# An instruction order planned by the kernel, quadrant tiles, and statistics turned on VectorE in a fused linear-attention and SoLU kernel

## The chip, the cores and the metric

The kernel runs on one core of a Trainium2 chip. The metric is the device time of one execution in microseconds (us). A run counts as slow when it lies over 1.5% above the fastest of the same kernel, and as fast otherwise. Times quoted are medians of all runs, ratios use fast runs alone.

A few names. PE is TensorE (matmuls), PEld its weight loads, DVE is VectorE, ACT is ScalarE, POOL is GpSimd, which also issues the loads, and SP issues the stores. PSUM is the memory that PE writes its products to; the kernel divides it into eight tiles of 128 x 512 fp32, called *banks* here. Each engine has a queue of instructions, waits on semaphores for the others, and takes its queue in the given order: in the kernel before, PE stands 7.03 us before a product whose operand has not landed (at 25.1 us), although operands of a later product in its queue were ready at 19.3. The *granted clock* is the share of full speed that PE was allowed to run at.

## The reference

```python
# batch 8, heads 8, sequence 576, head dim 64: 4608 tokens of 512
def attention(q, k, v, g_norm):
    kv = einsum('bhsd,bhse->bhde', k, v)          # no softmax: 64 x 64 per head
    out = einsum('bhsd,bhde->bhse', q, kv)
    rms = sqrt(mean(out * out, axis=-1) + 1e-06)   # over the 64 of one head
    return out / rms * g_norm

def feed_forward(x, w_in, w_out, g_ln):            # w_in 512 x 1024, w_out 1024 x 512
    h = x @ w_in
    e = exp(h - max(h)); sm = e / sum(e)
    solu = h * sm
    ln = (solu - mean(solu)) / sqrt(var(solu) + 1e-06) * g_ln
    return ln @ w_out
# the heads of the attention's result are put side by side to form x
```

All inputs and the output are float32.

## The kernel before

The tokens are worked in nine chunks of 512: chunk c below 8 is the first 512 tokens of batch c, chunk 8 the eight remainders of 64. For one chunk the kernel makes kv, turns q, multiplies q @ kv, divides by the root mean square (x), then makes h = x @ w_in, e = exp(h), u = h e, the sums of u, u² and e over the 1024 columns, and u @ w_out, scaled at the end by one number per token. w_out is centred beforehand: the column means weighted with g_ln are subtracted, so that the mean of u need not be.

These are the parts that the change touches:

```python
# loads: 512 rows of k, v, q per batch, and remainders of 64 rows on their own, in 128 B pieces
def load_rem(t, src, b):
    lo = (b % 2) * 64
    nc.gpsimd.dma_start(t[lo:lo + 64, b // 2], src[b, :, 512:S, :].rearrange("h s d -> s h d"))

# q @ kv: one matmul of K = 128 per head pair, with kv on the diagonal of a 128 x 128 tile, zeros beside it
nc.tensor.matmul(t[:, :], kvbd[:, c, p, :], q_sb[c][:, p, :], start=True, stop=True)

# statistics: 20 matmuls into four column groups, an eviction, and four fp32 matmuls that turn the sums
for n, (i, mov) in enumerate(todo):                 # 8 of u², 8 of u, 4 of e
    j = n % 4
    nc.tensor.matmul(t[32 * j:32 * j + 32, :], stat_sel[:, i, :], mov, ..., tile_position=(0, 32 * j))
nc.vector.tensor_copy(sums[:, :], t[:, :])
for m in range(4):
    nc.tensor.matmul(st_ps[:, m, :], sums[:, m * 128:(m + 1) * 128], stat_pick[:, :], ...)

# column means of w_out in full fp32
for f in range(NF):
    nc.tensor.matmul(mean[0][:, :], g_mean[:, f, :], w_out_f[:, f, :], ...)

# the order: each step of chunk c has slots 0 to 7; the other work is put into slots by hand,
# and the framework's scheduler may still move it
at(0, 2, kv_mm, 1)
...
for c in range(NC):
    for m in range(4):
        at(c + 1, 2 * m, out_half, c, m, 0)
        at(c + 1, 2 * m + 1, out_half, c, m, 1)
    at(c + 1, 1, stats, c)
```

The softmax here doesn't subtract the row's maximum and nothing guards it: scores larger than these inputs give would overflow.

## Time and profile before

| what | before |
|---|---|
| median time (3 runs) | 233.3 us (231.86 to 233.44) |
| span of the profiled run | 231.9 us |
| start of the column sums of chunk 0 | 61.15 us |
| stretches of chunks 1 and 2, sums to sums | 23.0 and 22.0 us |
| the three full chunks after those | 20.2 us each |
| sums of the last chunk to the end | 14.4 us |

The nine places where a chunk's column sums start on PE serve as landmarks throughout: from one to the next lies one chunk's worth of work. The prediction shows the busy time of each engine between them. Two rows of finer stretches, 65 to 75 us, come from the table of busy time by stretches: the stretch and its length, busy time and instruction count of PE, PEld, DVE, ACT and POOL, then PE's granted clock, the DMA share and GB/s.

```profile
65.00:70.00 5.00, 3.46 (x53) 2.20 (x53) 3.60 (x7) 3.20 (x7) 4.96 (x6) 0.94 1.63 178
70.00:75.00 5.00, 4.67 (x35) 1.92 (x35) 3.79 (x7) 3.30 (x7) 5.00 (x7) 0.71 1.41 190
```

POOL is full in both and PE has a gap of 1.5 us in the first; right after that the granted clock falls to 0.71 in the mean of 5 us. Cut finer, it is 0.50 from 69.6 to 72.8 us and 1.00 on both sides.

Two rows of the groups of instructions (line, engine, operation, shapes, count; busy time in all, mean ns of one) belong to the statistics before:

```profile
L253 DVE COPY sums<-sum_ps 128x512 f32<-128x512 f32 x9 | 6.2, 692 | 8.3 <-PE sum_ps L248 8.3
L264 DVE TENSOR_TENSOR sq<-st 128x8 f32<-128x8 f32 x9 | 4.6, 509 | 0.3
```

The eviction of the sums takes 692 ns. An operation on eight numbers per partition takes 509 ns on average.

### The profile page before, as it was taken

The numbers are of one execution on the slowest core, as the hardware profiler recorded it, in microseconds if no ns is written. First come the engines' busy times: TensorE is split into PE (matmuls) and PEld (weight loads), VectorE is DVE, ScalarE is ACT, GpSimd is POOL, SyncE is SP. The second block draws the span as 40 slices with busy tenths as digits, with TensorE's granted clock in tenths as the row PEclk, the third lists the DMA queues.
The fourth block names the chain that finished last, engine by engine and source line by source line (L and its number), as shares of the span: only waits on it lengthen the run. The fifth ranks groups of instructions, "written<-read, shape, count | busy, mean of one in ns | idle before, by whom it ended". The sixth has DMA issues, their size and how long they took to land.

```text
span 231.9 us, 3917 instructions
## 1 busy us (share of the span) xinstructions
PE 197.1 (85%) x1510; PEld 95.6 (41%) x1536; DVE 142.3 (61%) x254; ACT 120.9 (52%) x199; POOL 159.6 (69%) x165
## 2 busy tenths in 40 slices
PE   0241679997979998999999999999999999999971
PEld 0230343443444434445444544544455454454330
DVE  4320161579677756965975696597668758557341
ACT  2003452656467556576667657666667848624110
POOL 8643200999999999998658476665847757869500
PEclk9999999999997999999999999999999999999998
DMA  5999999399999999999211021021102202202225
GB/s 60 178 197 198 258 316 190 40 139 116 195 178 193 223 219 169 138 174 183 88 52 45 3 90 71 24 90 48 47 0 102 82 0 93 91 0 91 93 60 122
DMA packets 45682, 27.00 MB, mean 116 GB/s; under 512 B 14944, under 2 KB 40544, under 8 KB 45664
## 3 DMA queue, kind: packets, MB, share of 16 engines
q0 software_dynamic: 39216, 17.30, 57.5%
q1 hardware_dynamic: 6448, 9.44, 12.6%
q8 instruction: 12, 0.20, 0.4%
q14 instruction: 6, 0.05, 0.1%
HBM read 32.51 MB, written 9.44 MB: 181 GB/s over the span
## 4 chain that ended last, share of the span: by engine, by line
PE 58%; POOL 15%; DMA 13%; DVE 6%; ACT 4%; issue 3%; POOLq 0%
PE out_ps L283 21%; PE h_ps L226 18%; DMA w_out_f<-in_moe_w_out_dram 8%; POOL usq_sb L235 5%; DMA vs<-in_v_dram 4%; PE sum_ps L248 4%; PE mean_ps L305 4%; PE st_ps L260 3%; POOL es_sb L237 3%; PE s_ps L207 3%; PE qT_ps L181 2%; DVE sq L264 2%; POOL ks L73 2%; POOL qs L73 2%; ACT osq L203 2%
## 5 line engine op out<-in xcount | busy, mean ns | idle before, releaser
L235 POOL TENSOR_TENSOR usq_sb<-u_sb 128x512 bf16<-128x512 bf16 x72 | 75.0, 1044 | 32.8 <-DVE u_sb L234 32.5
L233 ACT ACTIVATE e_sb<-h_ps,zero_t 128x512 f32<-128x512 f32 x72 | 48.9, 684 | 60.0 <-PE h_ps L226 59.6
L226 PE MATMUL h_ps<-x_sb,w_in_sb 128*128 128x512 bf16 x279 | 76.0, 387 | 1.9 <-DVE x_sb L212 0.8
L283 PE MATMUL out_ps<-w_out_sb,u_sb 128*128 128x512 bf16 x274 | 72.5, 379 | 2.7 <-DVE ob L291 1.4
L234 DVE TENSOR_TENSOR u_sb<-h_ps,e_sb 128x512 bf16<-128x512 f32 x72 | 49.4, 688 | 36.0 <-ACT e_sb L233 36.0
L237 POOL TENSOR_TENSOR es_sb<-e_sb 128x512 bf16<-128x512 f32 x36 | 45.9, 1274 | 14.2 <-ACT e_sb L233 13.8
L226 PEld LDWEIGHTS <-w_in_sb 128*128 128x128 bf16 x288 | 27.9, 101 | 38.0 <-issue 10.7
L283 PEld LDWEIGHTS <-u_sb 128*128 128x128 bf16 x288 | 26.4, 98 | 32.6 <-issue 3.7
L203 ACT ACTIVATE osq<-o_ps,zero_t 128x512 bf16<-128x512 f32 x36 | 24.1, 679 | 16.3 <-remote 14.8
L212 DVE SCALAR_TENSOR_TENSOR x_sb<-o_ps,g_rep,rst 128x512 bf16<-128x512 f32 x36 | 26.8, 749 | 7.8 <-ACT rst L211 7.3
L209 ACT ACTIVATE lss<-s_ps,eps_t 128x512 f32<-128x512 f32 x36 | 24.4, 682 | 8.3 <-PE s_ps L207 8.2
L291 DVE TENSOR_SCALAR ob<-out_ps,rstd 128x512 f32<-128x512 f32 x36 | 26.1, 743 | 3.0 <-PE out_ps L283 2.3
L211 ACT ACTIVATE rst<-lss,zero_t 128x512 f32<-128x512 f32 x36 | 25.8, 721 | 2.3 <-DVE x_sb L212 1.4
L181 PE MATMUL qT_ps<-ident,qs 128*64 128x128 bf16 x256 | 12.5, 246 | 10.9 <-POOL ident masks.py:199 8.4
L181 PEld LDWEIGHTS <-qs 128*64 128x64 bf16 x256 | 9.5, 124 | 18.1 <-issue 9.0
L167 DVE CAST kvbd<-kv_ps 64x256 bf16<-64x256 f32 x16 | 6.7, 419 | 14.9 <-PE kv_ps L158 14.7
L207 PE MATMUL s_ps<-osq,head_mean 128*128 128x512 bf16 x36 | 14.4, 405 | 1.7 <-ACT osq L203 1.3
L149 PE MATMUL kv_ps<-vs,ks 128*64 128x64 bf16 x256 | 7.3, 210 | 8.7 <-DMA vs<-in_v_dram 8.6
L186 DVE COPY qT_sb<-qT_ps 128x1024 bf16<-128x1024 bf16 x18 | 12.3, 683 | 2.5 <-PE qT_ps L181 2.4
L196 PE MATMUL o_ps<-qT_sb,kvbd 128*128 128x512 bf16 x29 | 11.3, 405 | 2.9 <-DVE x_sb L212 1.5
L149 PEld LDWEIGHTS <-ks 128*64 128x64 bf16 x256 | 5.9, 123 | 17.3 <-issue 17.3
L253 DVE COPY sums<-sum_ps 128x512 f32<-128x512 f32 x9 | 6.2, 692 | 8.3 <-PE sum_ps L248 8.3
(49 smaller groups left out, 138.5 us busy)
## 6 DMA issues: line engine op xcount, KB each, us to landing
out_dram<-ob SPq DMA_DIRECT2D x32, 256.0 KB, 2.5
qs<-in_q_dram POOLq DMA_DIRECT2D x8, 512.0 KB, 8.6
ks<-in_k_dram POOLq DMA_DIRECT2D x8, 512.0 KB, 8.3
vs<-in_v_dram POOLq DMA_DIRECT2D x8, 512.0 KB, 9.8
w_out_f<-in_moe_w_out_dram POOLq DMA_DIRECT2D x1, 2048.0 KB, 19.2
w_in_sb<-in_moe_w_in_dram POOLq DMA_DIRECT2D x2, 512.0 KB, 12.4
out_dram<-ob SPq DMA_DIRECT2D x8, 128.0 KB, 2.3
krem<-in_k_dram POOLq DMA_DIRECT2D x8, 64.0 KB, 7.6
```

The source lines that it names most:

```text
L181: nc.tensor.transpose(t[hh * 64:hh * 64 + 64, pp, cols], qs[c][:, 2 * p + hh, j, :], ident[:, :])
L203: nc.scalar.activation(out=osq[:, :], in_=t[:, :], func=AF.Square, bias=zero_t[:, :])
L209: nc.scalar.activation(out=lss[:, :], in_=t[:, :], func=AF.Ln, bias=eps_t[:, :])
L211: nc.scalar.activation(out=rst[:, :], in_=lss[:, :], func=AF.Exp, scale=-0.5, bias=zero_t[:, :])
L212: nc.vector.scalar_tensor_tensor(out=x_sb[c][:, p, :], in0=o_ps.pop((c, p))[:, :], scalar=g_rep[:, :], in1=rst[:, :], op0=MUL, op1=MUL)
L226: nc.tensor.matmul(t[:, :], w_in_sb[:, dt, f * 128:(f + 1) * 128], x_sb[c][:, dt, :], start=(dt == 0), stop=(dt == NP - 1),)
L233: nc.scalar.activation(out=e[:, f % 2, :], in_=t[:, :], func=AF.Exp, bias=zero_t[:, :])
L234: nc.vector.tensor_tensor(out=u_sb[c][:, f, :], in0=t[:, :], in1=e[:, f % 2, :], op=MUL)
L235: nc.gpsimd.tensor_tensor(out=usq_sb[c][:, f, :], in0=u_sb[c][:, f, :], in1=u_sb[c][:, f, :], op=MUL)
L237: nc.gpsimd.tensor_tensor(out=es_sb[c][:, f // 2, :], in0=e[:, 0, :], in1=e[:, 1, :], op=ADD)
L283: nc.tensor.matmul(t[:, :], u_sb[c][:, f, m * 128:(m + 1) * 128], w_out_sb[:, f, :], start=(f == 0), stop=(f == NF - 1),)
L291: nc.vector.tensor_scalar_mul(out=ob[:, :], in0=t[:, :], scalar1=rstd_sb[c][:, m:m + 1])
```

## The change

The intent is to take instructions off PE, to relieve POOL, and to start earlier, with an order of instructions that the kernel plans itself:

- A planner (a greedy list scheduler with one duration per piece) fixes the order, and the framework's scheduler is off.
- k and v are loaded as 96 partitions of six rows, with no remainder; q's remainders sit in their own tile.
- q @ kv uses 64 x 64 quadrants of the PE array: no zero half.
- The sums are turned by DVE's 32 x 32 block transpose and four small fp32 matmuls per chunk.
- The column means use the reduced fp32 type.
- Two of eight squares of u move from POOL to ACT; matmuls on zeros keep PE busy during the first loads; banks are shared out anew.

```diff
+FP32R = mybir.dt.float32r
+class Plan:                                  # pieces with engine, length, rank, needs and buffers
+    def order(self):                         # earliest start first, then the lowest rank
...
+    ctx.enter_context(tc.manual_schedule())
+    banks = {"h": 2, "out": 2, "o": 2, "s": 1, "misc": 1}
...
-    w_out_f = big.tile([128, NF, d_model], FP32, name="w_out_f")
+    w_out_f = big.tile([128, NF, d_model], FP32R, name="w_out_f")
...
+    plan.add("warm", "pe", 5.2, -9.0, lambda: warm(12), first=[("s", "warm")])
...
+    def load_kv(name, src, b):
+        t = T[name, b] = tile_of((name, b), [S // 6, H, 6, D], BF16)
+        nc.gpsimd.dma_start(t.rearrange("p h i d -> p h (i d)"), src[b].rearrange("h (p i) d -> p h (i d)", i=6))
...
+                for hh in range(2):
+                    for z in range(2):
+                        rows = slice(64 * z, 64 * z + 64)
+                        nc.tensor.matmul(
+                            ts[z][hh * 64:hh * 64 + 64, pp, :, cols], kvd[rows, b, hh, 2 * hf + pp, :],
+                            T["qT", c, hf][rows, 2 * pp + hh, :, cols], start=True, stop=True)
...
+    def sums(c, part):                       # u, u², e: three pieces of the plan, not one
+        ...
+    def sums_turn(c):
+        nc.vector.transpose(t.rearrange("p a b c -> p (a b c)"), T["sum", c][:, :])
+    def stats_mm(c):
+        for g in range(4):
+            nc.tensor.matmul(t[32 * g:32 * g + 32, :, :], fold[:, :], T["sumT", c][:, :, g, 0:3], ...)
...
+            engine = "act" if f in (2, 6) and c > 1 else "pool"      # squares of u
...
+            dst = out.rearrange("(b s) d -> b s d", b=B)[:, 512:S, :].rearrange("b (p j) d -> j b p d", j=4)
...
+    for c in range(NC):
+        for part in range(3):
+            plan.add(("sums", c, part), "pe", (0.5, 0.5, 0.25)[part], r + 0.1 + 0.02 * part, ...)
```

## The prediction

> **What bounds the kernel now.** I read the page's engine shares first, then the table of busy time by stretches, then the timelines. The page says only that PE is the busiest engine and that POOL is second:
>
> ```profile
> PE 197.1 (85%) x1510; PEld 95.6 (41%) x1536; DVE 142.3 (61%) x254; ACT 120.9 (52%) x199; POOL 159.6 (69%) x165
> ```
>
> An average over stages hides the limits, so I cut the span at the nine places where the column sums of a chunk start (tile sum_ps in PE's timeline: 61.15, 84.15, 106.15, 126.34, 146.55, 166.73, 185.75, 203.19, 217.54). Columns: stretch, its length, then busy time of PE, PEld, DVE, ACT, POOL.
>
> ```profile
> 61.15:84.15 23.00, 20.81 (x179) 9.93 (x181) 16.36 (x27) 15.35 (x26) 22.90 (x26) 0.93 1.54 198
> 84.15:106.15 22.00, 20.35 (x171) 9.81 (x174) 15.62 (x26) 13.15 (x23) 21.90 (x24) 1.00 1.28 170
> 106.15:126.34 20.19, 19.96 (x170) 9.79 (x172) 14.56 (x26) 13.25 (x23) 14.18 (x14) 1.00 0.37 92
> ...
> 185.75:203.19 17.44, 17.25 (x111) 8.27 (x113) 11.75 (x21) 11.09 (x19) 12.86 (x12) 1.00 0.17 61
> 203.19:217.54 14.35, 14.29 (x84) 6.72 (x84) 9.27 (x16) 4.61 (x8) 11.64 (x12) 1.00 0.15 55
> 217.54:231.90 14.36, 7.92 (x52) 3.53 (x52) 4.27 (x9) 0.59 (x2) 0.60 (x1) 0.93 0.39 93
> ```
>
> The kernel has four regimes. From 106 to 217 us PE is full (19.96 of 20.19) and nothing else is: PE sets the rate, 20.2 us a chunk. From 61 to 106 us POOL is full (22.90 of 23.00): it squares u, adds e, and also issues loads; PE has gaps, and in the row 65 to 70 its granted clock fell to 0.94, in 70 to 75 to 0.71. Before 61 us lies the start, and the end has PE half idle. PE's timeline of the start and of the end:
>
> ```profile
> 13.68 1.07 PE L149 MATMUL kv_ps<-vs,ks 128*64 128x64 bf16 x32 [1.55 <-DMA vs<-in_v_dram]
> ...
> 25.11 0.29 PE L149 MATMUL kv_ps<-vs,ks 128*64 128x64 bf16 x3 [7.03 <-DMA vs<-in_v_dram]
> 25.34 0.61 PE L207 MATMUL s_ps<-osq,head_mean 128*128 128x512 bf16 x1
> ```
> ```profile
> 31.81 1.03 PE L226 MATMUL h_ps<-x_sb,w_in_sb 128*128 128x512 bf16 x2
> 33.06 1.06 PE L226 MATMUL h_ps<-x_sb,w_in_sb 128*128 128x512 bf16 x2 [0.22 <-DVE qT_sb L186]
> 34.68 3.75 PE L305 MATMUL mean_ps<-w_out_f,g_mean 128*128 128x512 f32 x4 [0.56 <-DMA w_out_f<-in_moe_w_out_dram]
> ```
> ```profile
> 220.92 1.02 PE L283 MATMUL out_ps<-w_out_sb,u_sb 128*128 128x512 bf16 x4
> 223.36 3.61 PE L283 MATMUL out_ps<-w_out_sb,u_sb 128*128 128x512 bf16 x16 [1.42 <-DVE ob L291]
> ```
>
> At the start, the squares of chunk 0 are ready by 19.3 us (ACT's four squares run 16.84 + 2.42), but the instruction order puts the kv product of batch 1 ahead of their head sums, and that waits until 25.1 for v of batch 1. So the first h matmul is at 31.8; then the fp32 column means take 8.9 us of PE (the chain's pieces 3.75+0.86+1.72+2.59), in h's way. At the end PE waits 1.42 us for a bank.
>
> **What the Trainium skill says.** "TensorEngine Tiling (Array Packing)", Tiling Modes / Key Properties, says that different tiles run matmuls in parallel and that a change of tiling mode drains the array. The trace agrees: 32 kv matmuls of 64 columns take 0.62 us on the chain, 19 ns each, where 64 columns at h's pace (512 in the 0.216 us below) would need 27 ns alone; and the 20 sums matmuls of 512 columns in four column groups take 1.19 us where 20 in a row at the 0.216 us seen for h (a start to start of 0.86 us for four) would take 4.3. No run yet shows quadrants (row and column halves together). "FP8 and Floating Point Precision", TensorE Precision Notes, gives true fp32 four passes and a reduced fp32 with truncation. The trace: 16 fp32 instructions for 8 calls, 8.9 us, 1.1 us per call or five times 0.216. "VectorE: DVE Perf Modes", The three transpose paths, says that DVE transposes in 32x32 blocks only, so the change needs its extra `fold` matmul; nothing in this trace shows its cost. "DMA: Bandwidth & Descriptors", Specifications, asks for at least 512 B a packet; before, 14944 packets are smaller, but the rows show 190 GB/s written as bf16 in every loading stretch, with or without remainders, so I expect little from larger packets.
>
> **The change, part by part (PE work of one steady chunk).**
> - h and out: unchanged, 64 x 0.216 = 13.8 us. s (head sums): 4 x 0.216 = 0.87, unchanged.
> - Sums 1.2: unchanged, though split in three.
> - q turns: 32 transposes of 64 weights took 2 x 0.57 = 1.14; now 16 of full width. The remainder chunk shows that form: 8 in 0.45. So 0.90. Saved 0.24.
> - o = q @ kv: 4 x 0.216 = 0.87; now 16 quadrant matmuls of 256 columns. Four at a time: 4 x 0.107 = 0.43, and a switch of mode in each half, about 0.1 (the kv and sums groups have gaps of that size about them): 0.55. Saved 0.3. The zero half of kv and its memsets go.
> - kv: 40 matmuls in 0.62 + 0.25 = 0.87; now 48 with K=96, at 19 ns 0.93. Lost 0.06. Its four copies are split over DVE and ACT (about 0.42 each by the present row).
> - Statistics: 8 fp32 instructions, 0.80; now a DVE transpose replaces the eviction copy (0.69 the same size, if it streams one element a cycle) and 4 small fp32 calls, about 0.25. Saved 0.55.
> Sum: 20.2 - 0.24 - 0.3 + 0.06 - 0.55 = **19.1 us a chunk**, if no other engine takes over.
>
> **The other engines in that chunk.** POOL: usq 6 x 1.044 (two squares go to ACT) + es 4 x 1.274 = 11.4, loads 3 x 0.92 and one q remainder 0.72 = 3.5: 14.9 us, from 13.5 + 5.0 = 18.5 before. ACT: 8 e + 12 of o + 2 squares at the 0.58 start to start of its timeline, 2 copies, rstd: 14.2. DVE: 8 x 0.62 + 4 x 0.67 + 4 x 0.67 + 2 x 0.62 + 2 x 0.4 + 0.6 + 1.0 = 14. All under 19.1, so PE stays the bound, and POOL stops being one.
>
> **The start.** v of batch 0 now lands with its remainder: 0.2 MB more is ahead of it, while the small packets behind it go, so about 14 us as now (13.7). kv 1.0, copies 0.9, q@kv 0.5: o at 16.5. Then ACT does 2 squares, 4 Ln, 4 Exp, 10 x 0.6 = 6 us with about 0.8 of filling, and the last x_mul 0.75: first h at **24**, from 31.8, because nothing waits for batch 1 in between. In chunk 0, ACT has 8 e and 12 of attention(1), 12 us, plus waits; DVE 8 u, 4 x, copies and 8 w_center of 0.74, 15 us, part of it after w_out lands (34.6 before; same bytes, so 33); POOL 13.5 + 2.8. PE has only 12. So chunk 1's h starts near 38 (before 53.3, found by counting 32 h matmuls), and sums(0) falls at about 42 instead of 61.15: **19 us gained**, of which 8 is the earlier first h, 7 the fp32r means (8 x 0.22 = 1.8 for 8.9), 4 the denser order. The warming matmuls use idle PE time and only keep early durations near 0.38 rather than 0.61 us.
>
> **The span, landmark by landmark.** sums(0) 42; +20.0 for chunk 1, which still has late w_center work on DVE (before 23.0): 62; +19.3 (before 22.0, POOL bound): 81.3; three at 19.1 (before 20.2): 138.6; the remainder chunk's stretch 18.4 (before 19.0; its q@kv in 128 small matmuls gives some back): 157.0; 16.9 (17.44): 173.9; 13.8 (14.35): 187.7; tail 12.8 (14.36: less the 1.42 wait, as the last two outputs use other banks, and one store instead of eight half stores): **200.5**. The profiled span is 1.4 below the median time (231.9 against 233.3), so the time is **202 us**.
>
> **The rivals.**
> 1. *The order misfires.* The planner's durations are constants (h 0.87 us, e 0.57); engines are strict queues, so a matmul placed just before its operand is ready stalls everything behind it. For it: the present order has such stalls (25.1 us, 92.9 us for a square). Against: its constants match start to start times in the trace within 10%. With 1 us of stalls a chunk: 210.
> 2. *POOL or DVE becomes the bound early.* Chunks 0 and 1 still have all eight squares on POOL (16.3 us with loads) and w_center on DVE; if sums(1) comes at 66 and not 62, 206. In steady chunks both have 4 us to spare, which speaks against it.
> 3. *Quadrants do not run side by side.* Then o is 16 x 0.107 = 1.7 instead of 0.55, 1.1 a chunk: 211. The two column groups in kv and q speak for side by side; row halves together are untried.
> 4. *The loads bind the start.* If the larger packets help, batch 0 lands at 11 and all moves earlier by 3 us: 199. If the DMA order delays q or k of batch 1, chunk 1 starts late: 206.
>
> **Range and chances.** The steady saving (some 1.1 x 7) and the start (19) are separate; the start rests on a view of clear idle time, so a net loss would need several rivals at once. Eight in ten: 194 to 212. Faster 0.96, same 0.03, slower 0.01.
>
> **What would show each step.** First h matmul at 24 and sums(0) near 42; no stretch with POOL over 95%; steady stretches of 19.1 with PE at 19 or so; the out of q@kv at 0.25 to 0.3 us a half; the means in 2 us; last out to end under 6 us. The prediction is wrong if a steady stretch is no shorter than 20 us with PE below 95% (order), or if q@kv costs over 1 us a chunk, or if the first h comes after 28.

## The result, and the profile after

The changed kernel is correct and takes **221.84 us** (220.5 to 223.1, 4 runs) against 233.37 us of the kernel before in the same rounds. The ratio is 0.9525, with a 95% interval of 0.9436 to 0.9615. Ratios are the mean time of one kernel's fast runs over the mean of the other's fast runs of the same rounds, so they are not quite the ratio of the medians quoted. It is faster, as predicted, but the gain is 11.5 us instead of 31, and 221.84 lies outside the range of 194 to 212. The profiled run of the changed kernel is its fastest, 220.5 us.

The page's engine shares of the changed kernel:

```profile
PE 188.8 (86%) x1669; PEld 85.8 (39%) x1695; DVE 137.7 (63%) x249; ACT 133.8 (61%) x227; POOL 131.8 (60%) x136
```

POOL lost 28 us of work and is no longer near full. PE lost only 8 us and has the same share as before. The same table by stretches as in the prediction, cut where the sums of each chunk start:

```profile
47.58:69.44 21.86, 20.80 (x180) 9.46 (x183) 16.32 (x29) 17.40 (x29) 16.48 (x17) 1.00 0.84 143
69.44:90.78 21.34, 20.07 (x178) 9.07 (x181) 15.67 (x27) 15.04 (x26) 14.71 (x16) 1.00 0.77 136
90.78:110.69 19.91, 19.06 (x174) 8.74 (x177) 13.92 (x25) 15.12 (x26) 14.54 (x16) 1.00 0.81 147
...
200.40:218.70 18.30, 7.22 (x52) 2.52 (x52) 4.56 (x10) 0.59 (x2) 1.41 (x2) 0.82 0.22 72
```

No engine is full any more: PE misses 0.85 us in a steady chunk of 19.91, and no other engine comes within 4 us of it. The end has become longer: 18.30 us from the last chunk's sums, with PE busy for 7.22 of them.

Where the time went, landmark to landmark (the last column is warm3_bank, the variant with the lowest median, explained with the experiments):

| stretch | before | predicted | changed | warm3_bank |
|---|---|---|---|---|
| start to sums of chunk 0 | 61.2 | 42 | 47.6 | 48.8 |
| chunk 1 | 23.0 | 20.0 | 21.9 | 21.4 |
| chunk 2 | 22.0 | 19.3 | 21.3 | 19.0 |
| the next three | 60.6 | 57.3 | 58.9 | 56.1 |
| then, with the remainder's q @ kv | 19.0 | 18.4 | 18.4 | 18.7 |
| next | 17.4 | 16.9 | 17.9 | 17.8 |
| next | 14.4 | 13.8 | 14.5 | 13.7 |
| sums of the last chunk to the end | 14.4 | 12.8 | 18.3 | 11.5 |
| span | 231.9 | 200.5 | 218.7 | 207.0 |

So the 18 us missing are three things: the start with chunk 1 (7.5), the full chunks 2 to 5 (3.6) with 1.7 in the thin chunks behind them, and the tail (5.5). The start comes from one profile of each kernel; how far such a profile can be trusted there is said at the head of the experiments on the start.

PE's timeline of the start (start, duration, instruction, what it waited for) answers to the rows shown in the prediction:

```profile
23.15 2.11 PE L365 MATMUL h_ps<-x_sb,w_in_sb 128*128 128x512 bf16 x8 [1.43 <-DVE x_sb L310]
25.25 0.95 PE L238 MATMUL misc_ps<-v_sb,k_sb 96*64 96x64 bf16 x48
...
30.34 0.41 PE L274 MATMUL o_ps<-qT_sb,kvd 64*64 64x256 bf16 x8
...
34.48 0.74 PE L472 MATMUL out_ps<-w_out_f,g_mean 128*128 128x512 f32 x2 [1.39 <-DMA w_out_f<-in_moe_w_out_dram]
...
36.03 0.84 PE L274 MATMUL o_ps<-qT_sb,kvd 64*64 64x256 bf16 x8
...
42.88 0.59 PE L365 MATMUL h_ps<-x_sb,w_in_sb 128*128 128x512 bf16 x2 [1.65 <-DVE x_sb L310]
```

The first h is at 23.15, where 24 was predicted. From there on it is late: the first half of q @ kv of chunk 1 runs at 30.34, the second at 36.03, and h of chunk 1 can go on only at 42.88, where the prediction had 38.

The end, from DVE's and SP's timelines and from the table of stretches:

```profile
208.24 1.41 DVE L494 TENSOR_SCALAR ob_sb<-out_ps,rstd 128x512 f32<-128x512 f32 x2 [0.69 <-ACT rstd L466]
209.56 1.40 DVE L494 TENSOR_SCALAR ob_sb<-o_ps,rstd 128x512 f32<-128x512 f32 x2
```
```profile
209.01 3.47 SPq L502 DMA_DIRECT2D out_dram<-ob_sb  x4
```
```profile
212.00:216.00 4.00, 0.00 (x0) 0.00 (x0) 0.00 (x0) 0.00 (x0) 0.00 (x0) 0.53 0.52 174
```

All four outputs of the last chunk wait for rstd, which comes after the last product. They are scaled one behind the other until 210.96, and all four stores go out together. From 212 to 216 nothing runs but these stores, with half of the DMA engines busy (0.52) at 174 GB/s.

### The profile page after: what moved, and what is told of

Its sections match the earlier page's. It is cut to its first block, busy times and chain, and to the rows that moved or that the text cites. A ratio compares the mean times of both kernels' runs of the same rounds, so it can differ in the third digit from the quotient of the medians.

```text
span 218.7 us, 4197 instructions
## 1 busy us (share of the span) xinstructions
PE 188.8 (86%) x1669; PEld 85.8 (39%) x1695; DVE 137.7 (63%) x249; ACT 133.8 (61%) x227; POOL 131.8 (60%) x136
## 4 chain that ended last, share of the span: by engine, by line
PE 63%; DVE 14%; ACT 9%; DMA 5%; issue 4%; POOL 1%; DVEq 1%; POOLq 0%; ACTq 0%
PE out_ps L487 24%; PE h_ps L365 23%; PE misc_ps L429 6%; DMA v_sb<-in_v_dram 5%; PE misc_ps L257 3%; PE s_ps L295 3%; PE o_ps L274 3%; DVE u_sb L380 3%; DVE x_sb L310 2%; DVE ob_sb L494 2%; DVE kvd L247 2%; DVE w_out_sb L478 2%; ACT lss_sb L299 2%; ACT e_sb L373 2%; ACT osq_sb L289 2%
## 5 line engine op out<-in xcount | busy, mean ns | idle before, releaser
L391 POOL TENSOR_TENSOR usq_sb<-u_sb 128x512 bf16<-128x512 bf16 x58 | 59.9, 1040 | 23.1 <-DVE u_sb L380 23.1
L494 DVE TENSOR_SCALAR ob_sb<-out_ps,rstd 128x512 f32<-128x512 f32 x34 | 24.9, 743 | 11.7 <-PE out_ps L487 10.2
L310 DVE SCALAR_TENSOR_TENSOR x_sb<-o_ps,g_rep,rst_sb 128x512 bf16<-128x512 f32 x34 | 25.4, 746 | 6.5 <-ACT rst_sb L303 6.4
L303 ACT ACTIVATE rst_sb<-lss_sb,zero_t 128x512 f32<-128x512 f32 x36 | 25.8, 722 | 0.6
L299 ACT ACTIVATE lss_sb<-s_ps,eps_t 128x512 f32<-128x512 f32 x34 | 23.2, 683 | 1.9 <-PE s_ps L295 1.9
L289 ACT ACTIVATE osq_sb<-o_ps,zero_t 128x512 bf16<-128x512 f32 x33 | 21.1, 684 | 3.7 <-PE o_ps L274 2.7
L249 ACT CAST kvd<-misc_ps 64x256 bf16<-64x256 f32 x16 | 5.9, 368 | 16.7 <-DVE kvd L247 16.3
L295 PE MATMUL s_ps<-osq_sb,head_mean 128*128 128x512 bf16 x34 | 12.9, 380 | 0.7 <-ACT lss_sb L299 0.7
L257 PE MATMUL misc_ps<-ident,q_sb 128*128 128x128 bf16 x120 | 9.5, 224 | 3.8 <-DMA q_sb<-in_q_dram 2.0
L261 DVE COPY qT_sb<-misc_ps 128x1024 bf16<-128x1024 bf16 x17 | 11.6, 679 | 0.4 <-PE misc_ps L257 0.4
L389 ACT ACTIVATE usq_sb<-u_sb,zero_t 128x512 bf16<-128x512 bf16 x14 | 10.1, 722 | 2.6 <-DVE u_sb L380 2.6
## 6 DMA issues: line engine op xcount, KB each, us to landing
w_in_sb<-in_moe_w_in_dram POOLq DMA_DIRECT2D x2, 512.0 KB, 13.8
```

The lines of the kernel that those rows point to most:

```text
L257: nc.tensor.transpose(t[:, h, y, :], src, ident[:, :])
L289: nc.scalar.activation(out=t[:, :], in_=T[("o", *i)].rearrange("p a b c -> p (a b c)"), func=AF.Square, bias=zero_t[:, :])
L299: nc.scalar.activation(out=t[:, :], in_=T["s", i][:, :], func=AF.Ln, bias=eps_t[:, :])
L303: nc.scalar.activation(out=t.rearrange("p a b c -> p (a b c)"), in_=T["lss", i][:, :], func=AF.Exp, scale=-0.5, bias=zero_t[:, :])
L310: nc.vector.scalar_tensor_tensor(out=T["x", c][:, 2 * hf:2 * hf + 2, z], in0=T["o", c, hf, z][:, :, :, :], scalar=g_rep[:, :], in1=T["rst" ...
L391: nc.gpsimd.tensor_tensor(out=dst, in0=src, in1=src, op=MUL)
```

## The experiments

In all, 18 variants ran, in five groups, each on a chip of its own. Each group shares the runs of the kernel before, and variants of different groups are best compared by their ratio to it. My theory was that three separate things hold the time: the cut of the last stores and the order of the last chunk, the split of the sums in every chunk, and the path of w_out at the start. The rivals were the copies of kv, wrong constants in the plan, the loads of batch 1 and the granted clock. The base of a variant is the changed kernel (0.9525) unless said otherwise. Results are correct except where said.

### The tail: two causes

**tail_first** puts the last chunk's sums and statistics ahead of most of its output products:

```diff
-            engine = "act" if f in (2, 6) and c > 1 else "pool"
+            engine = "act" if f in (2, 6) and c > 1 or (c, f) == (NC - 1, 7) else "pool"
-    parts[part] + ((parts[1] + parts[2] if c < NC - 1 else []) if part == 0 else [("sums", c, part - 1)]),
+    parts[part] + (parts[1] + parts[2] if part == 0 else [("sums", c, part - 1)]),
+   ... + ([("sums", c, 2)] if c == NC - 1 and (m, half) > (0, 1) else []),
```

> The changed kernel with the last chunk's sums and statistics ahead of its output products (last square on ACT). Theory A (the tail is long because rstd comes at 208.2 us, after the last product at 207.7, so all four stores of the last chunk start together): rstd comes 3 to 4 us earlier, stores are spread, the time falls by 3 to 5 us. Rival B (the stores move over only half of the DMA engines, 0.5 share, and 1.05 MB takes 7 us whenever it starts): the time falls by the shift of rstd at most, about 3 us, and the last store still lands 7 us after the first starts. Rival C (the tail is the last product and nothing else): no change within 1 us.

Measured: 219.55 us (219.04 to 220.1), ratio 0.9427. From the sums of chunk 7 to the end it takes 29.8 us instead of 32.8. So the order of the last chunk is worth 2 to 3 us: rstd no longer stands behind the last product. Two things changed in it, though: the last chunk's three groups of sums now also follow one another directly (203.86, 204.30 and 204.73 us), and that may carry part of the gain: in sum1 below, which joins the sums but doesn't put them ahead of the products, the tail is 15.0 us, against 14.4 here.

**store16** spreads the last chunk's tokens over the partitions the other way round, so that the slowest dimension of the store is 16 and not 8:

```diff
-            q_last[16 * b:16 * b + 16].rearrange("p h j d -> p h (j d)"),
+            q_last[b:128:8].rearrange("p h j d -> p h (j d)"),
-    cols = slice(0, 128) if c < B else slice(16 * b, 16 * b + 16)
+    cols = slice(0, 128) if c < B else slice(b, 128, 8)
-    ...[:, 512:S, :].rearrange("b (p j) d -> j b p d", j=4)
+    ...[:, 512:S, :].rearrange("b (p j) d -> j p b d", j=4)
```

> The changed kernel with the remainder rows laid out so that the last stores' slowest dimension is 16 and not 8; nothing else moves. Theory B (the dimension of 8 keeps the last stores on half of the DMA engines): share in the tail goes from 0.5 to about 1, last output to end falls from 7.7 us to about 4.5, time falls by 2 to 3 us. Theory A (all four start together; 190 GB/s is what stores get anyhow, as before with 16 engines): share rises but the time stays within 1 us.

Measured: 221.89 us (219.65 to 222.6), ratio 0.9511. The row of the table by stretches that answers to the one above:

```profile
212.00:216.00 4.00, 0.00 (x0) 0.00 (x0) 1.41 (x3) 0.00 (x0) 0.00 (x0) 0.77 0.77 247
```

The stores now begin 2 us later in this run, and still end earlier. In its DMA view the share is 0.9 at its height, at 328 to 388 GB/s in the best slices, where the changed kernel stays at 0.5 and at most 217. From the end of the last scaling to the end of the span it is 4.5 us (213.4 to 217.9) instead of 7.7. The cause is shown in the trace, but the median did not move: in the profiled run the sums of chunk 0 came 1.8 us later, and the timed runs scatter by 3 us. The mechanism is what the Trainium skill says in "DMA: Bandwidth & Descriptors", Why a DMA increments its semaphore by 16 and not by 1: the number of engines of a transfer is the largest number up to 16 that divides the slowest dimension of both its sides. With 8 there the trace shows half the engines, with 16 nearly all; it agrees.

### The steady chunk: the split sums

Three theories stood against each other for the 0.8 us by which a steady chunk (19.91 us) exceeds the prediction (19.1): the four copies of kv that take turns on DVE and ACT, the split of the sums into three pieces, and the durations that the planner believes.

**kv_act** puts all four copies of kv on ACT, which takes away the turn-taking:

```diff
-        if hh == 0:
-            nc.vector.tensor_copy(dst, src)
-        else:
-            nc.scalar.copy(dst, src)
+        nc.scalar.copy(dst, src)
```

> The changed kernel with all four copies of kv on ACT and none on DVE. Theory (DVE and ACT take turns on the one bank of kv, 1.65 us in a row after 0.6 us of waiting for DVE, and the bank is then wanted for the next q turn, so PE idles 0.48 us a chunk): the idle time before the q turn goes, a steady chunk falls from 19.9 to 19.4 to 19.5 us, time by 2 to 4 us. Rival (PE work alone sets 19.9, the wait is made up elsewhere): within 1 us; or slower by 1 to 3 us because ACT carries 0.7 us more in a chunk.

Measured: 221.63 us (220.28 to 222.7), ratio 0.9513: no change. PE's timeline shows why the wait for the copies was a symptom:

```profile
118.22 1.02 PE L484 MATMUL out_ps<-w_out_sb,u_sb 128*128 128x512 bf16 x4 [0.86 <-DVE ob_sb L491]
```

The wait for the copies of kv (0.48 us at the same place before) is gone, and PE waits 0.86 us for a bank that DVE has yet to empty in its place. The steady chunks now alternate between 18.41 and 21.15 us, so this one row is an example and not the rule of every chunk; their mean is 19.8.

**sum1** makes the 20 matmuls of the sums one piece of the plan again, as they were in the kernel before:

```diff
-        for part in range(3):
-            plan.add(("sums", c, part), "pe", (0.5, 0.5, 0.25)[part], ...)
+        plan.add(("sums", c, 2), "pe", 1.25, r + 0.1, lambda c=c: [sums(c, part) for part in range(3)],
+                 parts[0] + parts[1] + parts[2], ...)
```

> The changed kernel with the column sums of a chunk as one group of 20 matmuls, as in the kernel before, and not in three pieces with other work between. Theory (the three pieces change the tiling mode three times and keep DVE's queue, whose head is the transpose of the sums, waiting 1.3 us a chunk): a steady chunk falls from 19.9 to 19.3 to 19.5 us, rstd of the last chunk comes 1 to 2 us earlier, time falls by 3 to 5 us. Rival (sums cost the same wherever they are; the period is set by q@kv, kv copies and DVE's burst after the statistics): period within 0.2 us and time within 1.5 us.

Measured: **215.28 us** (214.75 to 216.43), ratio 0.9254: 6.6 us less than the changed kernel by the medians, 6.3 by the ratios. PE's timeline of the same place in the steady chunk, first of the changed kernel, then of sum1:

```profile
110.69 0.61 PE L429 MATMUL misc_ps<-u_sb,stat_sel 128*32 128x512 bf16 x8
111.23 0.41 PE L274 MATMUL o_ps<-qT_sb,kvd 64*64 64x256 bf16 x8
111.58 0.61 PE L429 MATMUL misc_ps<-usq_sb,stat_sel 128*32 128x512 bf16 x8
112.35 0.81 PE L487 MATMUL out_ps<-w_out_sb,u_sb 128*128 128x512 bf16 x3 [0.16 <-issue]
113.09 0.40 PE L429 MATMUL misc_ps<-es_sb,stat_sel 128*32 128x512 bf16 x4
...
119.23 0.61 PE L257 MATMUL misc_ps<-ident,q_sb 128*128 128x128 bf16 x8 [0.48 <-ACT kvd L249]
```
```profile
111.49 0.61 PE L429 MATMUL misc_ps<-u_sb,stat_sel 128*32 128x512 bf16 x8
111.93 0.60 PE L429 MATMUL misc_ps<-usq_sb,stat_sel 128*32 128x512 bf16 x8
112.36 0.39 PE L429 MATMUL misc_ps<-es_sb,stat_sel 128*32 128x512 bf16 x4
112.68 1.04 PE L365 MATMUL h_ps<-x_sb,w_in_sb 128*128 128x512 bf16 x4
```

Read the starts, not the durations, because matmuls overlap. In one group, the 20 matmuls take 111.49 to 112.68, 1.19 us. Split, they take 0.54 (110.69 to 111.23), 0.77 (111.58 to 112.35, with 0.16 of issue) and 0.34 (113.09 to 113.43, where the next group starts): 1.65 us. That is 0.46 us more for the same work. The rest of the 0.9 us is the wait of 0.48 us further down, which sum1 doesn't have: with the sums spread over 2.7 us, DVE, whose next instructions are the turn of the sums and the small statistics, stood 1.28 us and 0.66 us at the head of its queue, and everything behind came late. In sum1 a steady chunk takes 18.99 us with PE busy for 18.7: the prediction's 19.1. The profiled spans differ by 5.0 us: chunks 2 to 5 give 5.1 and the tail 3.3, but the sums of chunk 1 come 4.1 us later than in the profile of the changed kernel. That the split costs what it costs because PE changes its tiling mode is argued and not shown: no run separates it from other costs of a new group.

**durations** leaves the split and gives the planner the durations that the trace shows:

```diff
-        plan.add(("sums", c, part), "pe", (0.5, 0.5, 0.25)[part], ...)
+        plan.add(("sums", c, part), "pe", (0.65, 0.65, 0.45)[part], ...)
-        plan.add(("st_mm", c), "pe", 0.15, ...)
+        plan.add(("st_mm", c), "pe", 0.28, ...)
   # likewise o 0.45 for 0.25, exp 0.6, copies of kv 0.42 one after the other, stats 0.8, rstd 0.6
```

> The changed kernel with the planner's durations set to what the trace measured (q@kv 0.45 and not 0.25 us, sums 0.65/0.65/0.45, kv copies 0.42 one after another, statistics 0.8). With these its own clock says 19.9 us a steady chunk and a last store at 210 us, where the original constants say 18.85 and 198.6; the chip showed 19.9 and 211. Theory A (the changed kernel runs 20 us later than planned because pieces cost more than planned; the order itself loses little): time within 1.5 us of the changed kernel. Theory B (the order is wrong because it was made with wrong durations): time falls by 3 us or more.

Measured: 222.04 us (221.45 to 222.8), ratio 0.9536: no change in time, but the steady chunk falls from 19.91 to 19.27 us, with the sums still in three pieces:

```profile
111.80 0.62 PE L429 MATMUL misc_ps<-u_sb,stat_sel 128*32 128x512 bf16 x8
113.32 0.62 PE L429 MATMUL misc_ps<-usq_sb,stat_sel 128*32 128x512 bf16 x8
114.21 0.40 PE L429 MATMUL misc_ps<-es_sb,stat_sel 128*32 128x512 bf16 x4
```

Start to start the pieces still take 1.65 us (0.55, 0.54, and 0.56 with 0.16 of issue), but the wait of 0.48 us is gone. So of the 0.92 us by which a steady chunk of the changed kernel exceeds one of sum1, 0.64 go with an order made from truer durations, and 0.28 are left for the split. The edit loses elsewhere what it gains here:

```profile
25.77 0.95 PE L238 MATMUL misc_ps<-v_sb,k_sb 96*64 96x64 bf16 x48 [2.25 <-DMA v_sb<-in_v_dram]
```

In its order the kv product of batch 1 stands ahead of the first h and waits for v, so the first h is at 26.65 us and the sums of chunk 0 start at 51.55 (47.58 in the changed kernel); and the stretch with the remainder's q @ kv takes 19.95 us instead of 18.37. One order is better in the loop, the other at the start.

**sum1_oldstat** is sum1 with the statistics of the kernel before (an eviction copy and four fp32 matmuls on full-width weights):

```diff
-        nc.vector.transpose(t.rearrange("p a b c -> p (a b c)"), T["sum", c][:, :])
+        nc.vector.tensor_copy(t[:, :], T["sum", c][:, :])
-        for g in range(4):
-            nc.tensor.matmul(t[32 * g:32 * g + 32, :, :], fold[:, :], T["sumT", c][:, :, g, 0:3], ...)
+        for m in range(4):
+            nc.tensor.matmul(t[:, m, :], T["sumT", c][:, m * 128:(m + 1) * 128], fold[:, :], ...)
```

> The kernel with sums as one group, but the statistics turned as in the kernel before (eviction copy and 8 fp32 matmuls of 128 weights) and not by DVE's transpose and a fold. Theory (of the prediction: 0.80 us of PE against 0.25): a steady chunk 19.5 to 19.6 us in place of 19.0, time 4 to 5 us above 215.3. Rival (the small matmuls hide in waits): period within 0.2 us, time within 1.5 us.

Measured: 222.61 us (220.49 to 223.22), ratio 0.9531, which is 7.3 us more than sum1 by the medians and 6.5 us by the ratios. A steady chunk takes 19.70 instead of 18.99: 0.71 us for the statistics, where the prediction said 0.55. PE's busy time in it rises from 18.73 to 19.52, so it is work of PE and not a wait. The block transpose of 128 x 512 takes 713 ns on average, the eviction in its place 688. So in the loop this part of the change pays fully. The rest of the difference is less sure: of 7.7 us between the two profiled spans, 1.9 were there before the sums of chunk 1, where single profiles scatter.

### Two parts on the kernel before

**b_fp32r** changes the type of the column means in the kernel before, and nothing else:

```diff
-    w_out_f = big.tile([128, NF, d_model], FP32, name="w_out_f")
+    w_out_f = big.tile([128, NF, d_model], FP32R, name="w_out_f")
-    g_mean = big.tile([128, NF, 128], FP32, name="g_mean")
+    g_mean = big.tile([128, NF, 128], FP32R, name="g_mean")
```

> The kernel before with the column means in fp32r and not fp32; nothing else. Theory (of the prediction): 8 means take 2 us of PE and not 8.9, and the time falls by 5 to 7 us. Rival (POOL is the bound from 61 to 106 us and takes up what PE gains before it): sums of chunk 0 come 5 to 7 us earlier but sums of chunk 2 within 2 us of 106, and the time falls by 0 to 2 us.

Measured: 232.98 us (231.97 to 233.54), ratio 1.0002, with an interval of 0.9932 to 1.0073: nothing. The sums of chunk 0 come 4.3 us earlier (56.9), but the next stretch gives it back:

```profile
61.00:85.00 24.00, 19.19 (x155) 8.68 (x159) 14.95 (x24) 13.04 (x23) 23.92 (x27) 0.93 1.54 207
```

POOL is full, so starting a chunk earlier only made it wait for POOL later. By the sums of the last chunk 2.05 us of the 4.3 are left, and the tail takes another 1.7. In the changed kernel, where POOL is not full, the same change may be worth more; that was not measured by itself.

**b_order** switches off the framework's scheduler in the kernel before, so that its instructions run in the order in which the program has them:

```diff
+    ctx.enter_context(tc.manual_schedule())
```

> The kernel before with its instructions issued in program order, and not as the framework's scheduler moves them; nothing else. Theory (of the prediction: the start is lost to the order alone): first h at 24 to 26 us and not 31.8, time falls by 5 to 8 us. Rival (w_out lands at 34.6 and POOL is full from 61 to 106 us, so what the start gains is given back): first h early, but the sums of chunk 2 within 2 us of 106, and the time within 2 us.

Measured: 243.5 us (242.98 to 243.85), ratio 1.0457. The first h comes at 22.0 us, 9.8 us earlier, and the sums of chunk 0 still come at 61.7. So in this order an early first h brought the sums of chunk 0 no earlier, although the prediction counted 8 of its 19 us at the start for it. And the scheduler's order was not the kernel's weak point: without it the steady chunk takes 21.2 us instead of 20.2.

### The start: several small terms

First, how far one profile can be trusted here. Changed kernel, tail_first and store16 give PE the same order of instructions up to chunk 2. Yet the first h is at 23.15, 25.05 and 24.32 us in their profiles, and the sums of chunk 1 start at 69.4, 72.0 and 71.3. So a difference below some 2.6 us at that landmark, between two single profiles, shows nothing. Counted from the first h, the three agree better (46.3, 47.0 and 47.0 us), but sum1 and best_a, which share an order up to there too, differ even so (48.4 and 50.2). Part of the scatter may be the clock: stretches of about 3.4 us with a granted clock of 0.50 lie at other places in each profile (7.5 to 10.9 us in the changed kernel, 17.0 to 20.4 and 44.3 to 47.7 in tail_first).

**load_clock** lets the planner believe that the loads land later (as the trace shows), so that the column means get a later place in PE's queue:

```diff
-                queue = max(queue, t + length + 1.0) + load
+                queue = max(queue, t + length + 2.9) + load
-    plan.add("w_out", "pool", 0.9, -1.2, load_w_out, load=5.4)
+    plan.add("w_out", "pool", 0.9, -1.2, load_w_out, load=6.6)
```

> The changed kernel with the planner's clock of loads set to the trace (first landing 1.9 us later, w_out 1.2 us longer, so that it expects w_out at about 34 us and not 31). Theory (the column means are placed ahead of work that is ready, PE waits 1.39 us for w_out at 34.5 and the second half of chunk 1's attention starts late): chunk 1's h starts at about 40.5 instead of 42.9, time falls by 1.5 to 3 us. Rival (two banks for q@kv make the halves of the attention follow one another, whatever the means do): chunk 1's h stays at 42 to 43 and the time within 1 us.

Measured: 223.19 us (222.59 to 224.22), ratio 0.9598. h of chunk 1 goes on at 42.90, as in the changed kernel (42.88): the block of PE by the load of w_out is not what holds it.

**no_warm** takes the 39 matmuls on zeros away:

```diff
-    plan.add("warm", "pe", 5.2, -9.0, lambda: warm(12), first=[("s", "warm")])
-    for n, key in enumerate(...):
-        plan.add(("warm", n), "pe", 0.7, -9.0, lambda: warm(3, "misc"), [key], ...)
-    plan.add("warm2", "pe", 2.6, -9.0, lambda: warm(12), [("qT_mm", 0, 1)], ...)
```

> The changed kernel without the 39 matmuls on zeros that fill PE's idle time at the start. Theory (of the prediction: they use idle time and only keep early durations near 0.38 us): h products of the first chunks partly at 0.6 us, first h within 1 us, time within 1.5 us of 221.8. Rival (the granted clock matters at the start): sums of chunk 0 come 2 us or more later and the time rises by as much.

Measured: 224.8 us (224.63 to 225.68), ratio 0.9649, which is 3.0 us more than the changed kernel; the two intervals (0.9604 to 0.9693, and 0.9436 to 0.9615) just touch. PE's timeline:

```profile
25.18 0.59 PE L361 MATMUL h_ps<-x_sb,w_in_sb 128*128 128x512 bf16 x1 [2.81 <-DVE x_sb L306]
...
28.69 1.49 PE L234 MATMUL misc_ps<-v_sb,k_sb 96*64 96x64 bf16 x48
```

The first matmul of h takes 0.59 us where 0.38 is usual, and the 48 of kv take 1.49 us where the changed kernel needs 0.95. From the first h to the sums of chunk 1 it is 49.4 us, where the three profiles above have 46.3 to 47.0. That the first h is at 25.18 us is no effect of the edit: warmed runs have 23.15 to 25.05. So the warming seems to be worth about 3 us.

**best_a** combines the three edits that the trace supports: sum1, tail_first and store16. All variants from here on build on it.

> Candidate for the best version: sums as one group, the last chunk's statistics ahead of its output products, and the last stores over a dimension of 16. Theory (the three losses are separate: 6.5 us for the sums, 3 for the order of the tail, 3 for the half of the DMA engines, of which one group of sums has already taken 1.5 to 2): time 210 to 212 us. Rival (with statistics early the stores are spread, and the engines no longer matter): 212 to 214.

Measured: **212.54 us** (210.58 to 214.28, 6 runs, one of them slow), ratio 0.908, interval 0.9022 to 0.9138. The tail is 11.5 us instead of 18.3, and the steady chunk 19.0. The sums of chunk 1 come later than in the changed kernel, 74.4 for 69.4 (50.2 us for 46.3 from the first h): what is left lies there.

**best_bank** gives the second half of chunk 1's q @ kv other banks, so that it need not wait until x of the first half has been read:

```diff
-            tag = "out" if c == 0 and hf else "o"
+            tag = "out" if c < 2 and hf else "o"
```

> The candidate with the second half of chunk 1's q@kv in the two banks of out, idle at that time, and not in those of the first half. Theory (chunk 1's attention takes 12.5 us after its q is there because two banks make its halves follow one another): second q@kv of chunk 1 at 31 and not 36 us, chunk 1's h begins 2 us earlier, time 1 to 2 us under the candidate. Rival (ACT is full after q of batch 1 has landed, 16 operations of 0.6 us, or what is gained is lost to the later column means): chunk 1's h within 1 us of 43, time within 1 us of the candidate, or slower.

Measured: 213.37 us (211.26 to 216.91, two slow), ratio 0.9108: the same. The second half comes at 33.6 instead of 39.1 and h of chunk 1 about 2 us earlier, but the sums of chunk 1 no earlier (0.1 us). In this profile the first h was 1 us later than in best_a's, and the clock was 0.50 at another place (57.4 to 60.9 us), so a gain of some 1 us may be hidden.

**no_center** takes the whole path of w_out away. It gives a wrong result: w_out is loaded as bf16 straight into the tile of the products; there are no means and no centring.

```diff
-        nc.gpsimd.dma_start(w_out_f[:, :, :], moe_w_out.rearrange("(n p) d -> p n d", p=128))
+        nc.gpsimd.dma_start(w_out_sb[:, :, :], moe_w_out.rearrange("(n p) d -> p n d", p=128))
-    for f in range(NF):
-        plan.add(("w_mean", f), ...)
-        plan.add(("w_center", f), ...)
```

> Wrong result on purpose: w_out is loaded as bf16 straight into the tile that the out products read; there are no column means and no w_center, on top of best_a. If the w_out path holds the start, the first h matmul stays near 24.2, the block of PE at 34 to 36 us goes, chunk 1's first u comes right behind its e instead of at 52.3, sums(0) falls from 52.2 to 44 to 46, sums(1) from 74.9 to 64 to 66, and the time from 212.5 to about 203. If attention of batch 1 (ACT and its loads) holds it, sums(0) stays above 49 and sums(1) above 70, and the time is 208 or more.

Measured: 211.71 us (210.9 to 212.26), ratio 0.91. The sums of chunk 0 come 3.7 us earlier, those of chunk 1 2.2 us earlier (72.7), and the time is that of best_a. Counted from the first h, the sums of chunk 1 come 2.7 us earlier than in best_a, but only 0.9 us earlier than in sum1, which shares best_a's order. So the w_out path, my main theory of the start, fell: it had promised 203 us. One wait of PE in this run shows what stood in its place:

```profile
56.18 0.41 PE L271 MATMUL o_ps<-qT_sb,kvd 64*64 64x256 bf16 x7 [3.93 <-DVE x_sb L307]
```

PE stands 3.93 us before the second half of chunk 2's q @ kv. It needs banks that x of the first half still reads, and that x stands behind square, head sum, Ln and Exp in two other queues.

**no_center_bank** is the same with best_bank's edit (a wrong result as well).

> Wrong result on purpose: as no_center, and the second half of q@kv of chunk 1 uses the out banks, so that it needn't wait for x of the first half. If the bank wait and the w_out path hide each other, this gains 2 us or more over no_center (the last x of chunk 1 some 4 us earlier). If not, the two agree within 1 us.

Measured: 210.02 us (208.52 to 210.96), ratio 0.9018. The sums of chunk 1 come 2.1 us earlier than in no_center (70.6), and 2.3 us earlier counted from the first h (45.2 for 47.5). The second half of chunk 1's q @ kv runs at 33.4 us instead of 38.0. The wait of 3.93 us lies in chunk 2, which the edit doesn't touch; it falls to 0.77, but that half comes only 0.5 us earlier. So without the centring the bank is worth about 2 us by these two profiles; the intervals of the two times overlap. With the centring, no gain was seen.

**kvq1** loads k, v and q of batch 1 ahead of w_in:

```diff
-        at = b - 2.4 if b > 1 else (-2.0, -1.5)[b]
+        at = b - 2.4 if b > 1 else (-2.0, -1.9)[b]
-        plan.add(("q", b), "pool", 0.9, at + (0.1 if b else -0.1), ...)
+        plan.add(("q", b), "pool", 0.9, at + (0.05 if b == 1 else 0.1 if b else -0.1), ...)
```

> best_a with k, v and q of batch 1 loaded ahead of w_in. If their landing holds the start, q@kv of chunk 1 comes 3 us earlier, sums(0) and sums(1) with it, and the time is about 209.5. If the w_out path holds it, the first h comes later by the time of the loads moved ahead of w_in (up to 3 us) or not at all, and sums(1) stay at 74 to 76: time within 1.5 us of 212.5.

Measured: 211.57 us (211.38 to 211.96), ratio 0.9093: the same as best_a. q @ kv of chunk 1 comes 2.8 us earlier (28.54 for 31.37), the sums of chunk 1 1.5 us earlier (73.4), those of chunk 0 not at all; 1.5 us is within the scatter.

**warm3** puts eight more matmuls on zeros into PE's pause ahead of chunk 1's h:

```diff
+    plan.add("warm3", "pe", 1.7, -9.0, lambda: warm(8), [("s_mm", (1, 1, 1)), ("w_mean", 7)], first=[("s", "warm3")])
```

> best_a with eight more warming matmuls while PE waits for chunk 1's x. If the granted clock (0.66 in the stretches 35 to 40 and 45 to 50 us) costs time, the clock of 45 to 55 us is 1.00, h takes 0.86 instead of 1.46 for four, and the time falls by 1.5 to 2 us. If DVE's w_center sets the pace there, the time is the same within 1 us.

Measured: **210.6 us** (210.04 to 210.79), ratio 0.9045, interval 0.9004 to 0.9086. The same stretch of best_a, then of warm3:

```profile
45.00:50.00 5.00, 4.00 (x17) 1.85 (x17) 4.75 (x9) 0.80 (x2) 0.00 (x0) 0.66 1.20 171
```
```profile
45.00:50.00 5.00, 4.43 (x62) 2.44 (x56) 4.53 (x9) 2.12 (x4) 0.39 (x1) 1.00 1.09 153
```

The granted clock (third number from the end) is 1.00 instead of 0.66, which is the mean of a part at 0.50 (46.7 to 49.9) and parts at 1.00; PE gets through 62 instructions, not 17. A group of four products takes 1.03 us and not 1.91, and the sums of chunk 1 come 2.6 us earlier (72.3). Counted from the first h that is 46.8 us, 3.4 less than in best_a and 1.6 less than in sum1. That the clock stays up in this stretch is shown; what it is worth is not, since best_a's and warm3's intervals of time overlap.

**warm3_bank** joins this with the other bank for chunk 1:

> warm3 with chunk 1's second q@kv half in the out banks. If the low clock hid the bank wait, sums(1) falls from 72.3 to 70 to 71 and the time from 210.6 to about 209. If w_center takes its place as the wait, sums(1) stays at 72 and the time within 1 us of 210.6.

Measured: **210.0 us** (208.72 to 215.7, 4 runs, one of them slow), ratio 0.8999, interval 0.8897 to 0.91. The record's verdict is "unclear": the interval lies below 1, but is 2% wide; and it overlaps those of warm3 and best_a, so no gain over them is shown. The sums of chunk 1 come at 70.7, 1.6 us earlier than in warm3. By the expectation this would mean that the low clock had hidden the bank wait. But the 1.6 us are there before anything that the edit touches: the first h is at 23.25 us here and at 25.04 in warm3, where the clock was 0.50 from 13.8 to 20.6 us, during chunk 0's kv (1.49 us for 0.95). From the first h on the two take 47.0 and 46.8 us: the other banks brought nothing that can be seen. This is the last column of the table above. Three of its rows:

```profile
30.00:35.00 5.00, 3.76 (x35) 1.57 (x34) 1.72 (x4) 4.65 (x8) 5.00 (x6) 1.00 1.36 265
35.00:40.00 5.00, 2.49 (x22) 1.00 (x22) 3.79 (x6) 5.00 (x9) 4.79 (x6) 1.00 1.38 200
...
50.00:55.00 5.00, 3.45 (x19) 1.39 (x15) 4.96 (x8) 3.61 (x6) 2.53 (x4) 1.00 0.95 125
```

POOL is full in the first, ACT in the second, DVE in the third, while PE has gaps of 1.2, 2.5 and 1.5 us. Three engines take turns as the bound within 25 us.

**kvq1_warm3_bank** adds the earlier loads:

> The same with k, v and q of batch 1 loaded ahead of w_in. If the terms add up, sums(1) falls by 1.5 us more, to about 69, and the time to 207.5. If the start is bound by work in a row (two attentions, the means and w_center ahead of chunk 1's end), sums(1) is no earlier than in warm3_bank and the time 209 to 211.

Measured: 210.68 us (209.27 to 210.73), ratio 0.9027, interval 0.8929 to 0.9125, again "unclear". The sums of chunk 1 come at 72.6, later than without the earlier loads. No sum of the terms is seen. In this profile the clock falls to 0.66 in 25 to 30 and in 35 to 40; that the edit put a pause of PE where nothing warms it is likely and was not tested.

| variant | median us | ratio to before | first h at | sums of chunk 1 start at | from one to the other |
|---|---|---|---|---|---|
| changed kernel | 221.84 | 0.9525 | 23.2 | 69.4 | 46.3 |
| sum1 | 215.28 | 0.9254 | 25.1 | 73.5 | 48.4 |
| best_a | 212.54 | 0.908 | 24.2 | 74.4 | 50.2 |
| warm3 | 210.6 | 0.9045 | 25.0 | 71.8 | 46.8 |
| warm3_bank | 210.0 | 0.8999 | 23.3 | 70.2 | 47.0 |

The table gives the first matmul of the sums. The text on the variants of best_a gives the first one of u² instead, which is 0.44 us later in each of them. Both best_a and warm3_bank beat the changed kernel and the kernel before, by 9 to 12 us and by 21 to 22.

## Why the prediction was right or wrong

**Right.** The direction; the first h (24 predicted, 23.15 measured, and 24.3 and 25.1 in two other profiles of the same order); that POOL ceases to be a bound (60%); the turns of q (0.90 predicted, two times 0.45 measured); kv (0.93 against some 0.89); and the statistics (0.55 predicted, 0.71 measured by undoing them). The sum of a steady chunk, 19.1 us, is close to what PE needs when nothing disturbs it: sum1 takes 18.99. As written the sum gives 19.17, and part of the hit is luck, because errors cancel: the statistics saved 0.16 us more than predicted, q @ kv cost 0.14 more. The offset from the profiled span to the time, 1.4 us, was taken from two different runs; the profiled run itself took 233.9 us for a span of 231.9.

**Wrong in the steady chunk.** The step is "Sums 1.2: unchanged, though split in three". The split sums take 1.65 us of PE where one group takes 1.19, and in the planned order a wait of about half a us elsewhere in the chunk came with them, through DVE's queue. The prediction took the size of the sums as work that is conserved; a split of a tiled group is not. Undoing it gained 6.3 to 6.6 us in all. The wait, however, was the order's: durations, with the split kept, does without it and takes 19.27 us a chunk, so only 0.28 of the 0.92 us remain with the split in that order. So rival 1 (the order misfires, 210) came true in part, with nearly 1 us of stalls a chunk, and its counter-argument "its constants match ... within 10%" was wrong: the plan had 0.25 us for a half of q @ kv, 1.25 for the sums and 0.65 for the statistics, where durations had to put 0.45, 1.75 and 0.8 from the trace. The truer constants mended the loop and spoiled the start. The prediction's own sign for the order (a stretch of 20 us or more with PE below 95%) would have missed this: the stretch is 19.91 us, with PE busy for 95.7% of it.

The smaller term of q @ kv was too low as well: 0.55 predicted for the two halves, 0.35 and 0.34 measured, 0.69 in all. Rival 3 (quadrants don't run side by side) is refuted: 8 matmuls of 256 columns take 0.35 us, where one after the other they would take 8 x 0.107 = 0.86.

**Wrong in the tail.** The step is "tail 12.8 (14.36: less the 1.42 wait ... and one store instead of eight half stores)". It saw that one transfer replaces two and not how the new one is cut: half of the DMA engines serve it, and it takes 7.7 us behind the last scaling. It also didn't notice that in the planned order rstd comes behind the last product. Each was shown by one run, about 3 us of trace each (18.3 to 14.4 in tail_first, which joins the last sums too, and to 15.05 in store16), and both together bring the tail to 11.5. The gains don't add: sum1 alone has a tail of 15.0.

**Wrong at the start.** The step is "chunk 1's h starts near 38 ... and sums(0) falls at about 42". It added up each engine's work in chunk 0 (PE 12, DVE 15, ACT 12) and took the largest, as if the rest overlapped. Measured, h of chunk 1 goes on at 42.88, and the sums of chunk 0 start at 47.58. Chunk 1's attention is a chain: turn, copy, q @ kv, square, head sum, Ln, Exp, x. It takes 14.8 us from the start of the turn of q (28.05 to 42.88). That its two halves use the same two banks, and so follow each other, is part of it: with other banks for the second half, best_bank shortened the chain from 16.7 us in best_a to 13.1, but the sums of chunk 1 came no earlier. Its split of the gain also failed: b_order got the earlier first h and gained nothing by it (though its order differs in all else too); b_fp32r got the shorter means and lost them in the next chunk. The prediction's word on the warming, that it "only keeps early durations near 0.38", took some 3 us for a trifle.

**What stays open.** No single cause was found to hold the start, and its cause stays open. From the first h to the sums of chunk 1, the w_out path is worth 0.9 to 2.7 us and the granted clock 1.6 to 3.4 (against sum1 and against best_a, which have the same order up to there), the banks 2.3 without the w_out path, with nothing seen once the clock is up; the earlier loads move the first h itself and can't be told apart. Each is one profile against another, and two profiles of one order differ by 1.8 us in this measure. Together they leave chunk 1 at 70.2 where 62 was predicted. That POOL, ACT and DVE are each full in turn is shown; that their queues set the remaining 8 us is argued from it, and no run here takes that apart. How much of the changed kernel's gain is due to the planner alone was not measured either, since its order can't be had without its pieces.

## What to carry to other kernels

When PE works in tiling modes, keep the matmuls of one mode together: cutting one group of 1.2 us into three cost 0.46 us on PE itself, and the chunk 0.9 us in one order and 0.3 in another. A sum of engine times came within 0.2 us of a steady loop here, in part by errors that cancel, but not near a start or an end; there follow the chain of one chunk through the engines with its banks, and read what each store does behind the last instruction. A wait that a profile names may be a symptom: take it away, and look whether the time moves or only the name. And before you read a difference off two single profiles, look at two profiles of the same order: here their starts lay up to 2.6 us apart.

## What the Trainium skill lacked or had wrong

- "TensorEngine Tiling (Array Packing)", Key Properties, says that a change of mode drains the array, and gives no cost. Here the same 20 column-tiled matmuls took 1.19 us in one group and 1.65 in three, of which 0.16 are issue.
- "TensorE: Matmul & The Clock Gate", Part 1, lets the clock fall after an idle window of about 3.4 us, and doesn't say how much work keeps a window from being idle. In best_a PE was busy for 1.27 us of the 3.4 us before 36.3, with no pause over 2.13 us, and the granted clock was 0.50 from 36.4 to 39.6. So a thinly filled stretch was enough here. (The section on a second failure mode of the same page says that short pauses between groups can do it, without a measure.) Warming PE was worth about 3 us in no_warm; in warm3 the gain in time is within the intervals.
- "FP8 and Floating Point Precision", TensorE Precision Notes, names the reduced fp32 but no speed. Three column means started within 0.90 us, 0.30 each, where bf16 of the same size needs 0.216 and, in the kernel before, full fp32 1.1.
- "VectorE: DVE Perf Modes", The three transpose paths, gives a time for a 128 x 128 block of bf16 alone, and none for a block transpose of a whole bank into SBUF. It is 713 ns for 128 x 512 fp32; a copy of the same size takes 688 to 692.
- "SBUF — State Buffer", Terms, says that of DVE and GpSimd the loser of the shared ports blocks fully, for the whole of the other's instruction; what share of a tiny instruction's time that makes stands on no page. In no_center, the square of 128 x 8 numbers that takes 0.17 us at the end took 1.15 us, from 52.07 to 53.22, beside an addition on POOL from 51.91 to 53.19. This fits the mean of 509 ns in the kernel before; no run was made for it.
- "DMA: Bandwidth & Descriptors" had the rule on the number of engines right: a slowest dimension of 8 gave a share of 0.52, and 16 gave 0.9. The prediction had not looked it up.
